# Last down projection of an attention and feed-forward block: two of seven products split by a second Strassen level, one-bank PSUM tiles

## The chip, the cores and the metric

The kernel runs on one core of a Trainium2 chip. The metric is the device time of one execution in microseconds (us); the time stated for a kernel is the median of its runs. A profile of one execution shows when each engine was busy and what ended its waits. The engines are TensorE (PE, matrix products into PSUM), VectorE (DVE), ScalarE (ACT), GpSimd (POOL) and SyncE (SP), whose queue issues most DMA transfers. "PEld" is the loading of a matmul's stationary operand.

## The reference

The inputs are bfloat16: x is 2048 x 1024, the gate and up weights are 1024 x 3584, the down weight is 3584 x 1024. Cut to what matters here:

```python
xn = layernorm(x)
s = linear_attention(xn, wqkv, wo)            # 32 heads, then @ wo
h = silu(xn @ w_gate) * (xn @ w_up)           # 2048 x 3584
g = silu(h @ w_down)                          # 2048 x 1024
out = x + s * g
```

## The kernel before

The attention part comes first (to about 246 us of the profile) and leaves `s` in DRAM. The feed-forward part then takes the 2048 tokens in two passes of 1024. A pass has a gate/up stage, which makes the hidden tile `h` (28 chunks of 128 hidden columns, each for 1024 tokens), and a down stage, which multiplies `h` by the down weight and finishes the output rows.

All of these products use one level of Strassen's scheme in Winograd's form. In the down stage, the left operand is cut into A11, A12 (tokens 0 to 511 with the even and the odd chunks of `h`) and A21, A22 (tokens 512 to 1023), the weight into B11, B12, B21, B22 with 512 output columns. Seven products take the place of eight: M1 = A11 B11, M2 = A12 B21, M3 = S4 B22, M4 = A22 T4, M5 = S1 T1, M6 = S2 T2, M7 = S3 T3, with S1 = A21 + A22, S2 = S1 - A11, S3 = A11 - A21, S4 = A12 - S2 and corresponding weight sums T. The outputs are C11 = M1 + M2, C21 = M1 + M6 + M7 + M4, C22 = M1 + M6 + M7 + M5, C12 = M1 + M6 + M5 + M3. The weight sums were made by POOL in the first pass (`emit_T`, L298) and lie in DRAM (`wd_drams`).

The last pass's down stage is `emit_down_m` (L1300). It takes the products one after another in the order 1, 2, 7, 6, 5, 4, 3 (`M_ORDER`, L190). Each covers four row tiles of 128 tokens; a row tile is 14 matmuls of 512 columns, accumulated into one PSUM bank (`prod_t`, L1337). Product 1 and 2 share banks; ACT copies the result of product 1 into the SBUF tile KA before product 2 goes on top. Products 6, 4 and the final pieces use four single-bank PSUM tiles (`pps`, "dx", L944); products 7, 5 and 3 use two tiles of two banks each (`ppd`, "dz", L945; `d_banks`, L1344). A bank's tile is what the dependency tracking knows: a wait counts for the whole tile. After a row tile, DVE adds KA or KB (`add`, L1352), ACT applies silu (`silu`, L1355), and `fin` (L1108) multiplies by `s` and adds `x` in two DVE operations, stores the rows through SP's queue, and asks for the `x` and `s` rows of a later tile (`io_load`, five tiles ahead).

The order on PE, DVE, ACT and POOL is the order in which the code emits the operations; SP's queue works in order too. Weights stream through eight slots of 1 MB (`w_slot`, L210, pool `wgu`, `NPK` = 8) in the order of `w_seq`; `load_w_to(n)` issues loads up to the n-th entry, and a load waits on SP until the slot's last reader is done. In the last gate/up stage the loop at L1518 asks for the tile of eight entries ahead of key i, makes products a and b of a key (`emit_a`, L964, `emit_b`, L997) and evacuates them on DVE and ACT (`emit_evac`, L1008). The loop also takes six `deferred` output tiles of the first pass, whose stores go through POOL's queue. POOL has no other work in this stage.

The end of the kernel is the last row tile of product 3, which is split into 384 and 128 columns (L1421 to L1437) so that silu, `fin` and store of the first piece run beside the second.

Of the kernel before, what the change touches and what calls it, by code (L numbers as in the profile page):

```python
# [21 lines left out]
def kernel(  # L22
# [12 lines left out]
    P = 128  # L35
# [152 lines left out]
    passes = list(range(NPASS - 1, -1, -1))  # L188
    NWA = NFG // 2
    M_ORDER = (1, 2, 7, 6, 5, 4, 3)  # L190
    M_PACK = {1: ("a", 3), 5: ("a", 0), 6: ("a", 1), 7: ("a", 2), 2: ("b", 0), 3: ("b", 1), 4: ("b", 2)}
    w_seq = []
    for p in passes:
        for fg in range(NFG):
            w_seq.append((p, "g", fg))
            w_seq.append((p, "u", fg))
        if p == passes[-1]:
            w_seq += [(p, "m", (M, hf)) for M in M_ORDER for hf in range(2)]
            continue
        for kd in ("a", "b"):  # L200
            for j in range(NWA):
                w_seq.append((p, kd, j))
# [13 lines left out]
    def load_wd(t, k):  # L216
        for c, q in ((2 * k, 3), (2 * k + 1, 0)):
            nc.sync.dma_start(out=wd_q(t)[:, q], in_=wd_v[:, c, :])

    def raw_view(key, t):  # L220
        return wd_q(t)[:, 0:4:3, :] if key[1] == "w" else t[:, 0].rearrange("p a b -> p (a b)")
# [8 lines left out]
    def load_w():  # L230
        key = w_seq[w_next[0]]
        w_next[0] += 1
        if key in w_tiles:
            return
        p, kind, k = key
        t = w_slot()
        if kind in ("a", "b"):
            src = wd_drams[k][0 if kind == "a" else 1]
            nc.sync.dma_start(out=t[:].rearrange("p h a b -> p (h a b)")[:, 0:2 * WDN[kind]],
                              in_=src[:].rearrange("p k q n -> p (k q n)"))  # L240
        elif kind == "m":
            (M, hf), (kd, q) = k, M_PACK[k[0]]
            v = wd_q(t).rearrange("p q n -> p (q n)").rearrange("p (k n) -> p k n", n=CW)
            for j in range(NWA):
                k0, k1 = max(2 * j, NWA * hf), min(2 * j + 2, NWA * (hf + 1))
                if k0 < k1:
                    nc.sync.dma_start(out=v[:, k0 - NWA * hf:k1 - NWA * hf],
                                      in_=wd_drams[j][0 if kd == "a" else 1][:, k0 - 2 * j:k1 - 2 * j, q])
        elif key[1:] in pk_drams:
            gate([nc.sync.dma_start(out=t[:], in_=pk_drams[key[1:]][:])], first_gate[0], sync=True)  # L250
        else:
            load_gu(t, kind, k, first_gate[0])
            raw_keys.add(key)
        w_tiles[key] = t
# [684 lines left out]
    with ExitStack() as p3:  # L939
# [1 line left out]
        m4 = p3.enter_context(tc.tile_pool(name="p3m", bufs=4, reuse_waits="tile"))  # L941
        iop = p3.enter_context(tc.tile_pool(name="p3io", bufs=5, reuse_waits="tile"))
        hp = p3.enter_context(tc.tile_pool(name="p3h", bufs=1, reuse_waits="tile"))
        pps = p3.enter_context(tc.tile_pool(name="p3ps", bufs=4, space=PSUM, reuse_waits="tile"))  # L944
        ppd = p3.enter_context(tc.tile_pool(name="p3pd", bufs=2, space=PSUM, reuse_waits="tile"))  # L945

        def k2(shape, dt, name):
            return kp.tile(shape, dt, name=name, tag="k2")
# [117 lines left out]
        def emit_hs(h, hf, m, eng):  # L1066
# [13 lines left out]
            eng.tensor_tensor(out=a21.bitcast(F16), in0=a12, in1=S2, op=ALU.subtract)  # L1080
            s_ring[(hf, m)] = (S1, S2, S3)

        deferred = []
        io_tiles = {}

# [32 lines left out]
        def emit_down(p, h, base, last, more_S, next_S):  # L1118
# [51 lines left out]
            def evac_a(t, keep):  # L1170
                x_, y_, zw = bk[t]
                if keep:
                    st = xnp.tile([P, 3, CW], FP32, name="kept", tag="xn8")
                    s1, s3, u4 = [st[:, q, :] for q in range(3)]
                else:
                    s1 = k2([P, CW], FP32, "s1")[:]
                    s3 = k2([P, CW], FP32, "s3")[:]
# [122 lines left out]
        def emit_down_m(p, h, base):  # L1300
# [3 lines left out]
            S1, S2, S4 = [v.bitcast(F16) for v in (A21, A11, A12)]  # L1304
            s3_ = [xnp.tile([P, NWA, TB], F16, name="S3h", tag="xn8") for _ in range(2)]
            EV = (nc.vector, nc.vector, nc.sync)

            def S3(k):
                return s3_[k // NWA][:, k % NWA]
# [4 lines left out]
                v = {1: A11, 2: A12, 3: S4, 4: A22, 5: S1, 6: S2}[M]  # L1314
                return lambda k: v[:, k]

            def sums(out, a, b_, op, part=slice(0, NFG)):
                for k in range(part.start, part.stop, 2):
                    nc.vector.tensor_tensor(out=out(k), in0=a[:, k:k + 2], in1=b_[:, k:k + 2], op=op)

            def at(v):
                return lambda k: v[:, k:k + 2]

            def s3_sums():
                for k in range(NFG):
                    nc.vector.tensor_tensor(out=S3(k), in0=A11[:, k], in1=A21[:, k], op=ALU.subtract)

            def w_of(M, k):
                t = w_tiles[(p, "m", (M, k // NWA))]
# [8 lines left out]
                for k in range(NFG):  # L1338
                    mm(M, t, k, out, first)

            def s_banks():
                return [pps.tile([P, CW], FP32, name="dx", tag="s")[:] for _ in range(TPB)]

            def d_banks():  # L1344
                v = [ppd.tile([P, 2, CW], FP32, name="dz", tag="d") for _ in range(TPB // 2)]
                return [v[t // 2][:, t % 2] for t in range(TPB)]

            def kept(nm):
                v = [m4.tile([P, 2, CW], FP32, name=nm, tag="m4") for _ in range(TPB // 2)]
                return [v[t // 2][:, t % 2] for t in range(TPB)]  # L1350

            def add(out, a, b_):  # L1352
                nc.vector.tensor_tensor(out=out, in0=a, in1=b_, op=ALU.add)

            def silu(c, nm):  # L1355
                g_ = k2([P, CW], BF16, nm)[:]
                nc.scalar.activation(out=g_, in_=c, func=ACT.Silu, scale=rch)
                return g_

            def load(n):  # L1360
                load_w_to(base + 2 * n + NPK)


            load(0)
            E = s_banks()
            KA = kept("kA")
            for t0 in (0, 2):
                for k in range(NFG):
                    for t in (t0, t0 + 1):
                        mm(1, t, k, E[t], True)  # L1370
                if t0 == 0:
                    s3_sums()
                for t in (t0, t0 + 1):
                    nc.scalar.copy(out=KA[t], in_=E[t])
            load(1)
            sums(at(S1), A21, A22, ALU.add)
            g = []
            for t in range(TPB):
                prod_t(2, t, E[t], False)
                g.append(silu(E[t], "g11"))  # L1380
                if t == 0:
                    sums(at(S2), S1, A11, ALU.subtract)
                else:
                    fin(p, t - 1, 0, g[t - 1], *EV)
            load(2)
            fin(p, TPB - 1, 0, g[-1], *EV)
            O = d_banks()
            KB = kept("kB")
            for t in range(TPB):
                prod_t(7, t, O[t], True)  # L1390
                add(KB[t], O[t], KA[t])
                if t == 0:
                    sums(at(S4), A12, S2, ALU.subtract)
            load(3)
            E = s_banks()
            for t in range(TPB):
                prod_t(6, t, E[t], True)
                add(KB[t], E[t], KB[t])
                add(KA[t], E[t], KA[t])
            load(4)  # L1400

            def out_of(M, bank, K, t, row, cc, pre):
                c = k2([P, CW], FP32, "c%d" % M)[:]
                add(c, bank, K)
                g_ = silu(c, "g%d" % M)
                if pre is not None:
                    fin(*pre, *EV)
                return (p, row, cc, g_)

            pre = None  # L1410
            O = d_banks()
            for t in range(TPB):
                prod_t(5, t, O[t], True)
                pre = out_of(5, O[t], KB[t], t, t + TPB, 1, pre)
            add(KA[-1], O[-1], KA[-1])
            E = s_banks()
            for t in range(TPB):
                prod_t(4, t, E[t], True)
                pre = out_of(4, E[t], KB[t], t, t + TPB, 0, pre)
            fin(*pre, *EV)  # L1420
            hs_ = [slice(0, 3 * CW // 4), slice(3 * CW // 4, CW)]  # L1421
            ps = [pps.tile([P, CW], FP32, name="df%d" % i, tag="s")[:] for i in range(2)]
            for i in range(2):
                nc.scalar.copy(out=ps[i][:, 0:hs_[i].stop - hs_[i].start], in_=KA[-1][:, hs_[i]])
            pre = None
            for t in range(TPB - 1):
                prod_t(3, t, O[t], False)
                pre = out_of(3, O[t], KA[t], t, t, 1, pre)
            fin(*pre, *EV)
            t = TPB - 1  # L1430
            g12 = k2([P, CW], BF16, "g12")[:]
            for i, cs in enumerate(hs_):
# [7 lines left out]
        for pi, p in enumerate(passes):  # L1440
# [68 lines left out]
                emit_hs(h, 0, 3, nc.vector)  # L1509

            na0 = 6 if first else 8
            load_w_to(base + na0)
            if first:
                wd_pipe2(-1)
# [1 line left out]
            emit_c22(keys[0])  # L1516
            first_gate[0] = None
            for i in range(n):  # L1518
                load_w_to(base + i + (na0 if i < n - 7 else 8 if i > n - 6 or not first else 7))
                if i + 1 < n:  # L1520
                    emit_a(keys[i + 1])
                    emit_c22(keys[i + 1])
# [19 lines left out]
                if first:  # L1542
                    wd_pipe2(i)
                    if i == 5:
                        emit_lk(0)
                    if i == n - 5:
                        emit_lam()
                    elif i == n - 4:
                        emit_sc(keys[-1], w_tiles[keys[-1]])
                        emit_T(keys[-1], w_tiles[keys[-1]])  # L1550
                        scale_h(h, 1, nc.vector)
                    elif i == n - 3:
                        scale_h(h, 3, nc.vector)
                if deferred:
                    deferred.pop(0)()
            base += n
# [37 lines left out]
```

## Time and profile before

| what | us |
|---|---|
| runs | 762.24, 762.67, 763.14 (median 762.67) |
| the profiled execution: its own time | 762.88 |
| its span, first to last instruction | 761.1 |
| last gate/up stage in it (about) | 500 to 667 |
| last down stage: first matmul, end of the last one | 667.70, 757.22 |
| last DVE operation ends | 758.24 |

The page of the profile gives the busy time of each engine, the chain of work that ended last, and groups of instructions by source line, engine and operation. A group's line ends with count, busy time, mean duration of one and the idle time before it with what ended it. Matmuls are pipelined: a matmul of 512 columns shows a duration of 379 ns, but 112 in a row take 24.17 us, 0.216 us each. A timeline lists instructions in order of time, equal neighbours merged; brackets give the engine's idle time before and what released it.

### The profile page before, as it was taken

To read this page: it belongs to the slowest core of one execution; us is meant where nothing else is said; L and a number is where in the kernel's file an instruction comes from. 1 tells how busy PE (TensorE), PEld (TensorE's weight loads), DVE (VectorE), ACT (ScalarE), POOL (GpSimd) and SP (SyncE) were. 2 spreads that over 40 slices of the span, in tenths; PEclk is the share of its full clock that TensorE was granted. 3 is DMA by queue.
4 is the path that set the end of the run, shared out by engine and by line. 5 is a ranking of instruction groups with operands and counts; after the bars stand their busy time and mean duration, and the time that the engine had idled before them with its cause. 6 is when DMAs were issued, how large, how long until landed. Compare 5 with 4: busy or idle time off the path is not lost.

```text
span 761.1 us, 10540 instructions
## 1 busy us (share of the span) xinstructions
PE 750.4 (99%) x3731; PEld 348.7 (46%) x3731; DVE 557.4 (73%) x1018; ACT 376.7 (50%) x529; POOL 273.9 (36%) x348
## 2 busy tenths in 40 slices
PE   8999999999999999999999999999999999999997
PEld 3544444454544444444444444444444444444443
DVE  6687787886796788888889755478767676794344
ACT  5678776988956566666659201142232322221012
POOL 2444799998540275867665000110000000000000
PEclk9999999999999999999999999999999999999999
DMA  9966799879679667888899046498545444565321
GB/s 316 303 148 132 236 329 306 292 159 296 203 160 311 221 237 269 310 295 306 268 349 404 30 150 236 152 399 283 195 176 186 185 168 146 174 205 180 99 90 49
DMA packets 117269, 170.31 MB, mean 224 GB/s; under 512 B 35488, under 2 KB 95392, under 8 KB 107488
## 3 DMA queue, kind: packets, MB, share of 16 engines
q1 hardware_dynamic: 111568, 144.99, 59.2%
q0 software_dynamic: 4208, 22.15, 7.5%
q10 hardware_dynamic: 1440, 2.49, 0.9%
q8 instruction: 29, 0.48, 0.2%
q14 instruction: 24, 0.20, 0.1%
HBM read 111.67 MB, written 50.59 MB: 213 GB/s over the span
## 4 chain that ended last, share of the span: by engine, by line
PE 96%; DVE 2%; ACT 1%; DMA 0%; issue 0%; ACTq 0%; DVEq 0%
PE zw L952 25%; PE kv_ps L541 15%; PE xb L952 13%; PE yb L952 6%; PE q_ps L183 6%; PE dzw L1140 6%; PE dx L1334 6%; PE dz L1334 4%; PE dx L1140 3%; PE fx L803 3%; PE s_ps L761 2%; PE dy L1140 2%; PE kvz L563 1%; PE nd L730 1%; DVE w_sb L296 0%; PE fx L761 0%
## 5 line engine op out<-in xcount | busy, mean ns | idle before, releaser
L952 PEld LDWEIGHTS <-w_sb 128*128 128x128 f16 (+1 forms) x1568 | 152.2, 98 | 182.7
L952 PE MATMUL xb<-xnT,w_sb 128*128 128x512 bf16 x448 | 115.0, 379 | 0.0
L541 PE MATMUL kv_ps<-wkv_sb,xnT 128*128 128x512 bf16 x512 | 113.7, 379 | 0.6 <-ACT xnT L530 0.4
L952 PE MATMUL zw<-xnT,w_sb 128*128 128x512 bf16 x448 | 105.8, 379 | 0.0
L952 PE MATMUL zw<-S,w_sb 128*128 128x512 f16 x448 | 105.8, 379 | 0.0
L308 POOL TENSOR_TENSOR w_sb<-w_sb 128x512 f16<-128x512 bf16 x42 | 50.2, 1195 | 95.7 <-DVE w_sb L296 51.3
L273 ACT ACTIVATE w_sb<-w_sb 128x2048 bf16<-128x2048 bf16 x42 | 79.9, 1902 | 4.6 <-DMA w_sb<-in_B_w_up_dram 4.6
L541 PEld LDWEIGHTS <-xnT 128*128 128x128 bf16 x512 | 48.4, 98 | 55.9 <-ACT xnT L530 0.8
L183 PE MATMUL q_ps<-xnT,wq_sb 128*128 128x512 bf16 x256 | 58.4, 379 | 0.0
L1028 ACT ACTIVATE sg<-cg 128x1024 bf16<-128x1024 f32 x28 | 29.6, 1057 | 57.4 <-DVE cg L1021 57.4
L952 PE MATMUL yb<-S,w_sb 128*128 128x512 f16 x224 | 57.4, 378 | 0.0
L1021 DVE SCALAR_TENSOR_TENSOR cg<-zw,rc_all,s 128x1024 f32<-128x1024 f32 x28 | 35.9, 1284 | 25.6 <-PE zw L952 13.8
L1334 PEld LDWEIGHTS <-hT 128*128 128x128 f16 (+1 forms) x350 | 33.7, 98 | 42.0 <-issue 3.2
L980 DVE SCALAR_TENSOR_TENSOR s<-yb,rc_all,s 128x512 f32<-128x512 f32 x42 | 31.4, 749 | 28.0 <-ACT s L979 28.0
L309 POOL TENSOR_TENSOR w_sb<-w_sb 128x512 f16<-128x512 bf16 x42 | 50.5, 1201 | 3.3
L311 POOL TENSOR_TENSOR w_sb<-w_sb 128x512 f16<-128x512 bf16 x42 | 50.3, 1197 | 0.0
L310 POOL TENSOR_TENSOR w_sb<-w_sb 128x512 f16<-128x512 bf16 x42 | 50.2, 1196 | 0.0
L1334 PE MATMUL dx<-w_sb,hT 128*128 128x512 bf16 (+1 forms) x224 | 48.8, 379 | 0.0
L1114 POOL DMA_DIRECT2D out_dram<-io x16 | 8.7, 542 | 101.9 <-DVE io L1113 101.6
L1140 PE MATMUL dx<-w_sb,hT 128*128 128x512 bf16 x112 | 42.4, 379 | 0.0
L979 ACT ACTIVATE s<-xb,rcl 128x512 f32<-128x512 f32 x14 | 9.6, 687 | 65.3 <-PE xb L952 65.3
L979 ACT ACTIVATE s<-xb,rc_all 128x512 f32<-128x512 f32 x42 | 28.3, 674 | 21.8 <-issue 12.8
(192 smaller groups left out, 1172.2 us busy)
## 6 DMA issues: line engine op xcount, KB each, us to landing
w_sb<-pk_g SPq DMA_DIRECT2D x27, 1024.0 KB, 5.5
pk_g<-w_sb SPq DMA_DIRECT2D x14, 1024.0 KB, 5.1
w_sb<-pk_u SPq DMA_DIRECT2D x14, 1024.0 KB, 5.0
pk_u<-w_sb POOLq DMA_DIRECT2D x13, 1024.0 KB, 5.4
w_sb<-wd SPq DMA_DIRECT2D x42, 256.0 KB, 3.8
w_sb<-in_B_w_gate_dram SPq DMA_DIRECT2D x14, 512.0 KB, 6.7
w_sb<-in_B_w_down_dram SPq DMA_DIRECT2D x28, 256.0 KB, 4.5
w_sb<-in_B_w_up_dram SPq DMA_DIRECT2D x14, 512.0 KB, 5.4
```

The costliest lines, as they stand in the source:

```text
L183: nc.tensor.matmul(q_ps[:], lhsT=wq_sb[:, dc, g * P:(g + 1) * P], rhs=xn_ap(dc, btok), start=(dc == 0), stop=(dc == DC - 1))
L273: nc.scalar.activation(out=junk, in_=raw_view(key, t), func=ACT.Square, accum_out=asum[:])
L308: nc.gpsimd.tensor_tensor(out=T1, in0=b12, in1=b11, op=ALU.subtract)
L309: nc.gpsimd.tensor_tensor(out=T2, in0=b22, in1=T1, op=ALU.subtract)
L310: nc.gpsimd.tensor_tensor(out=T3, in0=b22, in1=b12, op=ALU.subtract)
L311: nc.gpsimd.tensor_tensor(out=T4, in0=b21, in1=T2, op=ALU.subtract)
L541: mm = nc.tensor.matmul(kv_ps[:], lhsT=xn_ap(dc, tok), rhs=wkv_sb[:, dc, c * CW:(c + 1) * CW], start=(dc == 0), stop=(dc == DC - 1))
L952: mm = nc.tensor.matmul(out, lhsT=lhs(k), rhs=rhs(k), start=(first and k == 0), stop=(k == HK - 1), skip_group_check=True)
L979: nc.scalar.activation(out=s1[:], in_=x_[:], func=ACT.Copy, scale=rc)
L1021: nc.vector.scalar_tensor_tensor(out=d12, in0=zw[:], scalar=rc, in1=s2[:, None, :].to_broadcast([P, 2, TB]), op0=ALU.mult, op1=ALU.add)
L1140: nc.tensor.matmul(out, lhsT=lhs, rhs=rhs, start=first, stop=lastk, skip_group_check=True)
L1334: nc.tensor.matmul(out, lhsT=lhs_of(M)(k)[:, t * P:(t + 1) * P], rhs=w_of(M, k)[:, cols], start=first and k == 0, stop=k == NFG - 1, skip_ ...
```

## The change

Products 2 and 4 of the last down stage are each computed by a second level of the same scheme. For a pair of row tiles, the left operand (7 pairs of chunks) is a 2 x 2 grid: row tile by even or odd chunk; the weight is cut into two halves of 256 columns. Seven products of 128 rows, 7 chunks and 256 columns replace eight, for each of the two pairs (`l2_p`): 98 matmuls of 256 columns in place of 56 of 512. Results and partial results of a pair lie in halves of two banks (`l2_M`); ACT copies a half bank where a partial result is needed twice.

The second-level weight sums are made in the last gate/up stage: in every third key SP loads parts of the first-level sums into a weight slot (`l2_load`), POOL makes four differences (`l2_sums`) and stores seven blocks to DRAM (`l2_drams`). The weight lead in this stage is therefore six slots in place of eight until key 24. POOL also makes the left-hand sums for product 2 there (`l2_lhs`, every fourth key) and those for product 4 in the down stage, into two SBUF tiles left from the first pass. The weight entries of products 2 and 4 become four slots each (two of the seven products in one slot).

The PSUM pools of four single-bank and two two-bank tiles are closed before the down stage, and one pool of eight one-bank tiles takes their place. The order of the work changes with it: the first row tile of product 7 lies inside product 2, that of product 3 inside product 4; tile finishes are collected in a list (`fins`) and emitted by `flush`. The order of `w_seq` by products stays.

```diff
+    L2 = (2, 4)
+    L2_ORDER = (1, 5, 2, 6, 7, 4, 3)
-            w_seq += [(p, "m", (M, hf)) for M in M_ORDER for hf in range(2)]
+            w_seq += [(p, "m", (M, q)) for M in M_ORDER for q in range(4 if M in L2 else 2)]
...
+        def l2_load():
+            M, j0 = l2_q.popleft()
+            kd, q = M_PACK[M]
+            t = w_slot()
+            v = t[:].rearrange("p h a b -> p (h a b)").rearrange("p (b j n) -> p b j n", b=8, n=CH)
+            js = range(j0, min(j0 + 2, NQ))
+            for j in js:
+                for k, b0, b1 in ((0, 0, 7), (1, 2, 6)):
+                    src = wd_drams[j][0 if kd == "a" else 1][:, k, q].rearrange("p (c n) -> p c n", n=CH)
+                    nc.sync.dma_start(out=v[:, b0:b1 + 1:b1 - b0, j - j0, :], in_=src)
...
+            for o_, a_, b_ in ((1, 7, 0), (3, 6, 1), (4, 6, 7), (5, 2, 3)):
+                nc.gpsimd.tensor_tensor(out=b(o_), in0=b(a_), in1=b(b_), op=ALU.subtract)
+            nc.gpsimd.dma_start(out=l2_drams[M][:, :, js.start:js.stop, :], in_=v[:, 0:7, 0:n_, :])
...
+            eng.tensor_tensor(out=s1, in0=a21, in1=a22, op=ALU.add)
+            eng.tensor_tensor(out=s2, in0=s1, in1=a11, op=ALU.subtract)
+            eng.tensor_tensor(out=s3, in0=a11, in1=a21, op=ALU.subtract)
+            eng.tensor_tensor(out=s4, in0=a12, in1=s2, op=ALU.subtract)
...
+            p3a.close()
+            ppm = p3.enter_context(tc.tile_pool(name="p3m8", bufs=2 * TPB, space=PSUM, reuse_waits="tile"))
...
+                for i, r in ((1, 0), (5, 0), (1, 1), (5, 1)):
+                    l2_p(M, i, r, A, bk)
+                for r in range(2):
+                    nc.scalar.copy(out=zy(r)[:, hi], in_=xw(r)[:, lo])
+                for r in range(2):
+                    l2_p(M, 2, r, A, bk)
+                    l2_p(M, 6, r, A, bk)
+                    nc.scalar.copy(out=zy(r)[:, lo], in_=zy(r)[:, hi])
+                    tt(K[2 * r][:, hi] if in_place else c[r][0][:, hi], zy(r)[:, hi], K[2 * r][:, hi])
+                for r in range(2):
+                    l2_p(M, 7, r, A, bk)
...
+                fill()
+                for r in range(2):
+                    l2_p(M, 4, r, A, bk)
...
+                    l2_p(M, 3, r, A, bk)
...
+            bk = banks()
+            E = [bk[2], bk[3], bk[0], bk[1]]
...
+            l2_M(4, quads(h, 1, 1), KB, done4, fill3, True)
+            out3(1)
+            flush(len(fins) - 1)
...
+            out3(2)
+            flush()
...
-                load_w_to(base + i + (na0 if i < n - 7 else 8 if i > n - 6 or not first else 7))
+                    load_w_to(base + i + (6 if i < 3 * len(l2_steps) else 8))
...
+                    if i % 3 == 0 and l2_q:
+                        l2_load()
+                    if i % 3 == 1 and l2_live:
+                        l2_sums()
+                    if i % 4 == 0 and i >= 4:
+                        l2_lhs(quads(h, 1, 0), i // 4 - 1, nc.gpsimd)
```

## The prediction

> **What bounds the kernel now.** I read the table of busy time by stage first, with stages cut at the last pass's borders, then the chain of waits of the last stage, then that stage's timeline engine by engine, and last the single rows that price the new operations. TensorE (PE) is busy 99% of the span, so the question is where in the last down projection it isn't streaming.
>
> ```profile
> span 761.1 us, 10540 instructions
> PE 750.4 (99%) x3731; PEld 348.7 (46%) x3731; DVE 557.4 (73%) x1018; ACT 376.7 (50%) x529; POOL 273.9 (36%) x348
> ...
> 246.00:415.00 169.00, 169.00 (x803) 76.79 (x801) 142.41 (x237) 110.68 (x123) 111.11 (x111) 1.00 0.82 293
> ...
> 500.00:667.00 167.00, 167.00 (x775) 75.73 (x774) 123.97 (x151) 50.64 (x72) 3.24 (x6) 1.00 0.58 208
> 667.00:761.10 94.10, 86.31 (x411) 39.38 (x408) 48.86 (x96) 15.05 (x24) 0.00 (x0) 0.99 0.38 123
> ```
>
> The columns are the stretch, its length, then busy us of PE, PE's weight loads, DVE, ACT, POOL, then PE clock, DMA share and GB/s. Row one is the first pass's gate/up stage, row two the last pass's, row three the last down stage. PE is full in both gate/up stages; POOL is idle in the last two. In the last stage PE loses 7.8 us, and the chain says where:
>
> ```profile
> 667.87 24.17 PE dx L1334 x112
> 692.04 3.04 PE dz L1334 x14
> 695.08 0.02 issue
> 695.10 0.70 DVE kB L1353
> 695.80 0.04 issue
> 695.85 6.22 PE dz L1334 x28
> ```
>
> The columns are start, length, what. After each first tile of a product in the two-bank "dz" tiles PE stands until a DVE addition has read that bank, because the second bank belongs to the same tile. It happens five times (695.1, 702.1, 721.1, 728.1, 747.2). By issue times one costs more than the 0.78 us shown idle:
>
> ```profile
> 691.88 3.19 PE L1334 MATMUL dz<-w_sb,S3h 128*128 128x512 f16 x14
> 695.85 6.20 PE L1334 MATMUL dz<-w_sb,S3h 128*128 128x512 f16 x28 [0.78 <-DVE kB L1353]
> ```
>
> **Part 1: 112 matmuls of 512 columns become 196 of 256.** Products 2 and 4 are 56 matmuls each now; 112 take 24.17 us in the chain, 0.216 each. Two-level, each is 7 products x 2 row tiles x 7 chunks = 98 matmuls of 256 columns. No 256-column row exists. Below, half of 0.216 is 0.108. Above, a matmul of 384 columns: the last product's first 14 take 2.29 us, 0.1636 each. Its last 14, of 128 columns, run from 756.45 to 757.22, 0.055 each, though every weight load lasts 98 ns: loads hide even there. The middle of 0.055 and 0.1636 is 0.109, which I take, as 256 lies between these two rows. 196 x 0.109 = 21.4, a gain of 2.8 us. Bounds: 3.0 us gained (0.108) or 7.9 lost (0.1636).
>
> ```profile
> 754.16 2.29 PE df L1334 x14
> 756.45 0.02 issue
> ...
> 757.26 0.37 ACT L1436 ACTIVATE g<-df,hsc 128x128 bf16<-128x128 f32 x1 [0.20 <-PE df L1334]
> ```
>
> The Trainium skill, "TensorE: Matmul & The Clock Gate", section Back-to-back issue gap, speaks against this: it gives streams of weight load plus matmul a sustained 81 ns at 128 columns and says the plain N/2.4 + 2.5 ns under-counts small ones. If its 26 ns excess over this trace's 55 held at 256 columns, 196 x 0.026 = 5.1 us would more than eat the gain and the sum would read 763.4. The same section gives 131 ns at 512, where this trace has 216; the measurement decides.
>
> **Part 2: the five stalls.** The 14 matmuls from 691.88 would end their issue 3.02 us later; PE restarts 3.97 later: 0.95 lost. The pair from 695.85 restarts after 6.98 instead of 6.04: 0.94. Five make 4.7 us. With one-bank tiles the next tile of products 7, 5 and 3 waits for no evacuation of its neighbour, so I count all 4.7.
>
> **Part 3: what PE waits for instead.** (a) The new pool of one-bank tiles gives the second tile of product 1 a bank of the last "zw" pair. Its second matmul so waits for DVE's last evacuation:
>
> ```profile
> 667.90 1.28 DVE L1021 SCALAR_TENSOR_TENSOR cu<-zw,rcl,s 128x1024 bf16<-128x1024 f32 x1 [0.65 <-PE zw L952]
> ```
>
> It ends at 669.18; with a hand-over of 0.06 (695.79 to 695.85 above) PE goes on at 669.24 where it would have issued at 667.92: 1.32 us lost. All 55 matmuls left of that half-product's stream, and every later one, stand behind it. (b) In products 2 and 4, the third group (product 7 of the second row pair) waits for an ACT copy of half a bank and then a DVE addition from the same bank. The copies of 128 and 384 columns take 0.253 and 0.470, so 256 about 0.36; the additions of 512 and 1024 columns take 0.69 and 1.22, so 256 about 0.43. With hand-overs of 0.03, 0.03 and 0.06 and 0.16 until the last result lands (379 ns duration against 0.216 pitch) the chain is 1.07 us; the first pair's seven matmuls cover 0.76. 0.31 lost, twice: 0.6. Bounds: 0 (copy and addition overlap) and 2.1 (no cover). Less than nothing is excluded, since nothing before this group gets shorter.
>
> **Part 4: the tail.** DVE's stores are put off: after product 4 six output tiles wait to be multiplied and stored ("fin": two DVE operations each), and five of them are queued between the additions of tiles 1 and 2 of product 3. A burst in the pass before prices one:
>
> ```profile
> 481.70 0.42 DVE L1112 TENSOR_TENSOR g<-g,io 128x512 bf16<-128x512 bf16 x1
> 482.15 0.42 DVE L1113 TENSOR_TENSOR io<-g,io 128x512 bf16<-128x512 bf16 x1
> 482.50 0.42 DVE L1112 TENSOR_TENSOR g<-g,io 128x512 bf16<-128x512 bf16 x1
> ```
>
> 0.80 each. Counted from tile 1's result: addition to 0.64, five fins to 4.64, addition of tile 2 to 5.33, its silu on ACT (0.72) to 6.08, the fin before it to 6.05, its own to 6.91, the two last pieces (1.15, as from 757.09 to 758.24) to 8.06. PE is done 3.02 + 2.29 + 0.77 = 6.08 after the start, so DVE ends 1.98 behind PE, against 1.02 now (757.22 to 758.24). 1.0 us lost; bounds 0, and 1.8 if a fin takes the 0.93 it has here when each waits for its silu. The inputs of the burst's first fin are asked for behind the store of the fin in product 4's middle, 0.3 + 1.7 + 0.8 + 3.4 = 6.2 us (issue, landing, two issues, landing), some 8 us ahead. The stores (1.7 us to landing) and the end behind the last one stay.
>
> **Part 5: costed at nothing.** POOL gets, in the last gate/up stage, 32 sums on weights and 28 on activations, and 28 more in the down stage, for which it has until product 4's second group. At 1.2 us a 128x512 sum (its rows: 1195 to 1201 ns) and about 0.7 for half of that, 54 us fit in 167; the last 28 need 20 us and have 33. SP issues 28 more loads of 128 KB in that stage and 8 fewer for products 2 and 4; POOL issues 8 more stores, and six leftover output stores of the first pass stand behind its sums, with SP's reloads behind those and the gate/up weights behind them on SP. The cover is lead: with 6 slots ahead a weight tile is asked for four keys of 167/28 = 5.96 us, 24 us, before use, and lands in 5.5. A POOL step (4 x 1.2 + 0.6 = 5.4 us) is inside it. DMA grows by about 12.8 MB, 77 GB/s over 208, near the first gate/up stage's 293, where no PE wait is listed. Without this cover each us late is a us on the end. DVE's other sums move but end 4 us or more before PE needs them: after product 2 DVE owes seven sums of 0.61 us, and product 6, which reads them, is three tiles (9.1 us) away. With the stalls gone DVE has 3.0 us a tile for at most 2.1 us of additions and fin, so nothing is late next there.
>
> Here the Trainium skill, "SBUF — State Buffer", on the shared port pair, warns that a DVE operation with two SBUF inputs and a GpSimd operation block each other for a whole instruction. In this trace DVE's hT product keeps 952 to 959 ns whether POOL is busy 111 us of the stage or 3; only POOL stretches, 1142 to 1600 ns in one row.
>
> **Sum.** PE: -2.8 - 4.7 + 1.3 + 0.6 = -5.6. Tail: +1.0. Together -4.6 on the profiled execution's own 762.88 us (span 761.1 and 1.8 around it), which lies 0.2 above the median of 762.67 and inside the runs' 762.24 to 763.14: 758.3.
>
> **The rivals.** *Half-width matmuls cost more than half* (slower). One mechanism, the pitch in products 2 and 4: at 0.1325 the gain is gone, from 0.140 on the kernel is slower by over 0.2%, at 0.1636 it ends at 769.0. For it: no such matmul in the trace. Against: 0.055 at 128 columns under the same loads. Chance 0.07. *POOL takes DVE's time in the last gate/up stage*: 54 us of sums, if each held DVE, against 43 us of DVE idle: 11 over, 769. Against: the first gate/up stage, with twice the POOL work and a fuller DVE. Slower from 6 us over. Chance 0.06. *New waits and tail at their upper bounds*: +1.5 and +0.8, 760.6, still faster; additions on busy queues speak for it. Chance 0.16. *The stalls stay* (another dependency takes the bank's place): 763.0, no change. The order of waits speaks against it. Chance 0.07. *The forecast*: 0.64.
>
> About 0.2% (1.5 us) is what a measurement can tell from no change. Faster: 0.64 + 0.16 = 0.80; the same: 0.07 and a little of the first rival, 0.08; slower 0.12. The range: low 756.9, (b) and the tail near zero; high 761.6, beyond the upper waits and into the first rival at a pitch of 0.126.
>
> **What the profile after would show.** Right: 196 matmuls on one line with about 272 ns each and 98 of them in 10.7 us; no 0.78 us gap behind a kB or c addition; one 1.1 to 1.3 us PE gap behind "cu" just after the last gate/up matmul; two of about 0.3 behind the l2c and kB additions; DVE ending 2 us after PE; PE full in the last gate/up stage with POOL near 57 us. Wrong: the 98 taking 12 us or more; a PE wait on POOL or on a weight load; DVE ending 3 us behind.

## The result, and the profile after

The changed kernel takes 758.0 us in the median of four runs (757.58 to 758.68), the kernel before 762.89 in the same series: a ratio of 0.9938 (95% interval 0.9921 to 0.9955). A second series gave 757.94 (five runs) and 0.9935 (0.9921 to 0.9949). The forecast was 758.3. The profiled execution took 757.71 us, its span is 755.9.

The head of the profile of the changed kernel:

```profile
span 755.9 us, 10887 instructions
PE 746.6 (99%) x3815; PEld 356.8 (47%) x3815; DVE 573.5 (76%) x1036; ACT 379.5 (50%) x537; POOL 361.1 (48%) x444
```

The same stages as before, after the change (stretch, length, then busy us of PE, its weight loads, DVE, ACT and POOL, then PE clock, DMA share and GB/s):

```profile
246.00:415.00 169.00, 169.00 (x803) 76.78 (x802) 143.25 (x237) 110.92 (x124) 111.27 (x111) 1.00 0.81 291
500.00:667.00 167.00, 166.67 (x773) 75.54 (x772) 126.38 (x150) 50.49 (x72) 60.79 (x70) 1.00 0.75 267
667.00:755.90 88.90, 82.87 (x493) 47.45 (x491) 64.37 (x113) 16.82 (x32) 27.35 (x32) 1.00 0.52 165
```

POOL now works 61 us in the last gate/up stage and 27 us in the last down stage. PE is idle for 6.0 us of the last row, most of it behind its last matmul. And it is no longer full in the last gate/up stage: 0.33 us are missing, which the forecast did not have. The chain of waits of the last stage, after the change (start, length, what):

```profile
667.57 1.29 DVE cu L1035
668.86 0.04 issue
668.90 12.03 PE dm L1400 x55
680.93 6.13 PE dm L1433 x56
687.06 0.02 issue
687.08 0.37 ACT dm L1455
687.45 0.02 issue
687.47 0.44 DVE l2c L1388
687.91 0.04 issue
687.95 0.92 PE dm L1433 x7
688.88 3.02 PE dm L1400 x14
691.90 3.06 PE dm L1433 x28
694.95 33.24 PE dm L1400 x154
```

The pieces behind "kB" and "c" additions in the middle of a product are gone: 154 matmuls of products 7, 6, 5 run as one piece of 33.24 us. In their place stand the two waits that the forecast named: "cu" ahead of product 1's second matmul, and ACT's copy with DVE's addition ahead of the third group of product 2 (product 4 shows the same at 734.34). The 56 matmuls of 256 columns take 6.13 us, 0.109 each.

I cut the last part of each profile at three points: the first matmul of the last gate/up stage (498.49 us before, 497.66 after), the first matmul of the down stage (667.70 and 667.36) and the end of DVE's last operation (758.24 and 753.41). Before, the gate/up stage takes 169.21 us and the down stage 90.54; after, 169.70 and 86.05. The down stage got 4.49 us shorter, the gate/up stage 0.49 longer. The rest of the 5.2 us of span lies elsewhere: the code ahead of 498 us, which the change does not touch, ended 0.83 sooner, and the time from there to the last record of the trace fell from 2.84 to 2.53 us. The first of the two is a difference between executions: over all profiles of this study that point lies between 497.66 and 498.98. I therefore compare stages below, and use whole times as a check. That the whole came within 0.3 us of the forecast is in part luck: the sum has neither this difference, nor the shorter end, nor the loss in the gate/up stage, and the last offsets part of the others.

Two of the signs that the forecast named look otherwise: the waits on half banks show 0.14 us of idle time each, not 0.3 (by the starts of the matmuls on both sides they cost 0.30, since 0.41 us lie there in place of 0.11), and PE is not full in the last gate/up stage, where POOL has 61 us in place of 57.

### The profile page after: what moved, and what is told of

It is laid out like the page before. It is cut to its first block, busy times and chain, and to the rows that moved or that the text cites. A ratio compares the mean times of both kernels' runs of the same rounds, so it can differ in the third digit from the quotient of the medians.

```text
span 755.9 us, 10887 instructions
## 1 busy us (share of the span) xinstructions
PE 746.6 (99%) x3815; PEld 356.8 (47%) x3815; DVE 573.5 (76%) x1036; ACT 379.5 (50%) x537; POOL 361.1 (48%) x444
## 4 chain that ended last, share of the span: by engine, by line
PE 96%; DVE 2%; issue 1%; DMA 0%; ACT 0%; DVEq 0%; ACTq 0%
PE zw L966 25%; PE kv_ps L554 15%; PE xb L966 12%; PE q_ps L183 7%; PE dm L1400 7%; PE dzw L1204 6%; PE yb L966 6%; PE dx L1204 3%; PE s_ps L774 3%; PE fx L816 3%; PE dm L1433 3%; PE dy L1204 2%; PE nd L743 1%; PE kvz L576 1%; DVE g L1176 1%
## 5 line engine op out<-in xcount | busy, mean ns | idle before, releaser
L1122 POOL TENSOR_TENSOR w_sb<-w_sb 128x512 f16<-128x512 bf16 (+3 forms) x32 | 34.6, 1103 | 61.0 <-DMA w_sb<-wd 52.3
L1400 PE MATMUL dm<-w_sb,hT 128*128 128x512 f16 (+3 forms) x238 | 49.2, 366 | 1.2 <-DVE cu L1035 1.2
```

Of the source, the lines that this page charges most:

```text
L1400: nc.tensor.matmul(out, lhsT=lhs_of(M)(k)[:, t * P:(t + 1) * P], rhs=w_of(M, k)[:, cols], start=first and k == 0, stop=k == NFG - 1, skip_ ...
```

## The experiments

My theory is the sum on record: five gaps gone (-4.7), half-width matmuls (-2.8), the cu wait (+1.3), two half-bank waits (+0.6), the tail (+1.0). The rival to it is that the gain has one source, with the other terms as by-products. A second question is the 0.49 us in the gate/up stage, which none of these terms has.

| kernel | time, us (median) | ratio to before, 95% interval | last gate/up stage, us | down stage to DVE's end, us | behind it, us |
|---|---|---|---|---|---|
| before (its first profile) | 762.67 to 763.09 | 1 | 169.21 | 90.54 | 2.84 |
| changed (first series) | 758.0 | 0.9938 (0.9921 to 0.9955) | 169.70 | 86.05 | 2.53 |
| changed, once more | 757.94 | 0.9935 (0.9921 to 0.9949) | 169.22 | 86.03 | 2.55 |
| one-bank tiles only | 759.58 | 0.9955 (0.9942 to 0.9967) | 169.22 | 87.14 | 2.82 |
| one-bank tiles, product 1 by tiles | 758.18 | 0.9938 (0.9925 to 0.9950) | 169.21 | 85.83 | 2.82 |
| changed, product 1 by tiles | 757.07 | 0.9920 (0.9908 to 0.9933) | 169.71 | 84.72 | 2.54 |
| changed, tail dealt out | 757.21 | 0.9924 (0.9912 to 0.9936) | 169.21 | 84.96 | 2.54 |
| changed, 60 of POOL's sums left out | 758.69 | 0.9939 (0.9925 to 0.9953) | 169.21 | 86.03 | 2.86 |
| all three losses mended | 755.04 | 0.9898 (0.9885 to 0.9912) | 169.27 | 83.06 | 2.54 |
| the same, sums begun later | 755.17 | 0.9899 (0.9886 to 0.9913) | 169.22 | 83.05 | 2.54 |

**The one-bank tiles alone.** The products stay as before; only the pools change.

```diff
-        pps = p3.enter_context(tc.tile_pool(name="p3ps", bufs=4, space=PSUM, reuse_waits="tile"))
-        ppd = p3.enter_context(tc.tile_pool(name="p3pd", bufs=2, space=PSUM, reuse_waits="tile"))
+        p3a = ExitStack()
+        pps = p3a.enter_context(tc.tile_pool(name="p3ps", bufs=4, space=PSUM, reuse_waits="tile"))
+        ppd = p3a.enter_context(tc.tile_pool(name="p3pd", bufs=2, space=PSUM, reuse_waits="tile"))
...
-            def s_banks():
-                return [pps.tile([P, CW], FP32, name="dx", tag="s")[:] for _ in range(TPB)]
-            def d_banks():
-                v = [ppd.tile([P, 2, CW], FP32, name="dz", tag="d") for _ in range(TPB // 2)]
...
+            p3a.close()
+            ppm = p3.enter_context(tc.tile_pool(name="p3m8", bufs=2 * TPB, space=PSUM, reuse_waits="tile"))
+            def s_banks(n=TPB):
+                return [ppm.tile([P, CW], FP32, name="dm", tag="m")[:] for _ in range(n)]
+            d_banks = s_banks
...
-            E = s_banks()
+            bk = s_banks()
+            E = [bk[2], bk[3], bk[0], bk[1]]
...
```

> The kernel before, with its products as they are (512 columns, no second level), and only the PSUM pools of the last down stage exchanged for one pool of eight one-bank tiles, as the change has it. Theory (parts 2 and 3a of the prediction): the five gaps of 0.78 us behind kB and c additions go, five times 0.94 to 0.95 of issue is 4.7 us gained; the second matmul of product 1 now waits for the last cu evacuation, 1.3 us lost; together -3.4, so 759.5 us against the 762.9 of the kernel before, and the changed kernel is only about 1.3 us faster than this one (half-width matmuls -2.8, waits on half banks +0.6, tail +1.0). Rival: the gain of the change comes from the half-width products, the gaps are a matter of DVE and stay or move: no more than 1 us faster than before.

It took 759.58 us, and its down stage 87.14, 3.40 less than before. The chain of waits of this kernel:

```profile
667.74 1.30 DVE cu L1022
669.03 0.04 issue
669.08 83.82 PE dm L1335 x391
752.89 0.02 issue
752.92 0.59 ACT g L1439
```

After the cu wait PE streams to the end without a stop. The rival falls: the gaps were a matter of the two-bank tiles, and most of the gain is there without any second level. The changed kernel's down stage is 1.1 us shorter than this one's, near the 1.2 that the other terms sum to (-2.8 + 0.6 + 1.0).

**Product 1 tile by tile**, so that the bank of the last zw pair is needed 14 matmuls later.

```diff
-                for k in range(NFG):
-                    for t in (t0, t0 + 1):
-                        mm(1, t, k, E[t], True)
+                for t in (t0, t0 + 1):
+                    prod_t(1, t, E[t], True)
```

> The changed kernel with product 1 computed tile after tile instead of two tiles alternating, so that the bank which the last zw pair held is first needed 14 matmuls (3.0 us) later than now. Theory (part 3a): the 1.3 us gap behind the last cu evacuation goes and nothing takes its place: last stage 1.3 us shorter than the changed kernel's 83.95 us from its first matmul to PE's end, 756.6 us in all. Rival: the gap only moves, because product 1's first tile then also waits for a bank that is evacuated late (an ACT copy or the cu itself): no change.

The down stage took 84.72 us, 1.33 less than the changed kernel's 86.05, and the time was 757.07. The chain of waits across the border, in this kernel:

```profile
666.73 1.73 PE zw L966 x8
668.46 12.09 PE dm L1400 x56
```

The cu evacuation has left the chain; product 1 follows the last gate/up matmul. Against the kernel before in its own series the median gains 6.02 us, where the changed kernel gained 4.89. The two profiled executions differ by 0.3 us only (757.40 and 757.71), because this one began its last gate/up stage 0.92 us later; both have a gate/up stage of 169.7.

**The tail dealt out.**

```diff
+            flush(2)
             out3(1)
-            flush(len(fins) - 1)
+            flush(3)
```

> The changed kernel with the five held-back output tiles of the tail dealt out differently: two are finished before product 3's tile 1 is issued (so ahead of its addition in DVE's queue) and three after it, instead of five between the additions of tiles 1 and 2. Theory (part 4): DVE's lag behind PE at the end falls from 2.1 us to about 1.0, what the kernel before has, and the time by 1.0 to 756.9 us. Rival: the lag is that of the last tile's own chain (silu, two multiplications, two last pieces) and not of the burst: no change, or the burst is only met earlier and holds a PE bank.

In the changed kernel, the timeline of DVE (start, length, operation, and in brackets the idle time before it) ends with no idle moment from the addition of tile 2 on:

```profile
749.92 0.68 DVE L1388 TENSOR_TENSOR c<-dm,kA 128x512 f32<-128x512 f32 x1
750.52 0.41 DVE L1176 TENSOR_TENSOR g<-g,io 128x512 bf16<-128x512 bf16 x1
...
752.26 0.35 DVE L1176 TENSOR_TENSOR g<-g,io 128x384 bf16<-128x384 bf16 x1
752.65 0.36 DVE L1177 TENSOR_TENSOR io<-g,io 128x384 bf16<-128x384 bf16 x1
752.92 0.22 DVE L1176 TENSOR_TENSOR g<-g,io 128x128 bf16<-128x128 bf16 x1
753.18 0.23 DVE L1177 TENSOR_TENSOR io<-g,io 128x128 bf16<-128x128 bf16 x1
```

PE's last matmul ends at 751.31 there, so DVE is 2.10 us behind. With the tail dealt out:

```profile
751.41 0.36 DVE L1176 TENSOR_TENSOR g<-g,io 128x384 bf16<-128x384 bf16 x1 [0.50 <-ACT g L1568]
751.80 0.36 DVE L1177 TENSOR_TENSOR io<-g,io 128x384 bf16<-128x384 bf16 x1
752.08 0.22 DVE L1176 TENSOR_TENSOR g<-g,io 128x128 bf16<-128x128 bf16 x1
752.33 0.22 DVE L1177 TENSOR_TENSOR io<-g,io 128x128 bf16<-128x128 bf16 x1
```

DVE waits for the last tile's silu again, ends 1.02 us behind PE (751.53), as in the kernel before, and the down stage takes 84.96 us, 1.09 less. The lag came from the burst.

**POOL's sums left out.** The 32 sums on weights and the 28 for product 4's left operand go, so this kernel does not compute these operands; the 28 for product 2 stay, and so do matmuls, evacuations and stores. POOL's busy time in the last gate/up stage falls from 60.8 to 26.8 us.

```diff
-                for k, b0, b1 in ((0, 0, 7), (1, 2, 6)):
+                for k, b0, b1 in ((0, 0, 7), (1, 2, 6), (0, 1, 3), (1, 4, 5)):
...
-                nc.gpsimd.tensor_tensor(out=b(o_), in0=b(a_), in1=b(b_), op=ALU.subtract)
+                pass
...
-            for j in range(NQ):
-                l2_lhs(quads(h, 1, 1), j, nc.gpsimd)
```

> The changed kernel with POOL's second-level sums left out: the four differences of weight blocks in every step of the last gate/up stage (the blocks are loaded as they are, by two more loads a step) and the second round of sums on activations in the down stage (product 4 takes product 2's sums). So this kernel does not compute those operands; its matmuls, evacuations and stores are those of the changed kernel. Theory: the sums of POOL slow DVE operations with two inputs beside them (0.42 us fins at 1.26 to 1.36 in the last gate/up stage, 0.69 us sums at 1.1 in the down stage), which costs a PE wait of 0.33 us and some 0.5 us of that stage and nothing in the down stage, where DVE has room: DVE's durations fall back, the gate/up stage falls from 169.7 to 169.2 us and the time by 0.5 to 757.5 us. Rival: the 0.5 us is run to run difference of the stage and has nothing to do with POOL: DVE durations may fall, the time doesn't. Second rival: POOL's sums cost in the down stage too: 1 us or more.

This answered half. DVE's durations fell back as the theory had it, but for one hT product of 1.20 us in the last gate/up stage, where product 2's sums are still made. Groups of DVE instructions in the down stage (line, operation, shapes, count, busy us, mean ns, idle us before), of the changed kernel:

```profile
L1388 DVE TENSOR_TENSOR hT<-hT 128x1024 f16<-128x1024 bf16 x14 | 11.4, 881 | 0.0
...
L1388 DVE TENSOR_TENSOR hT<-hT 128x1024 f16<-128x1024 f16 x7 | 7.4, 1125 | 0.0
```

and without POOL's sums:

```profile
L1388 DVE TENSOR_TENSOR hT<-hT 128x1024 f16<-128x1024 bf16 x14 | 8.6, 679 | 0.0
...
L1388 DVE TENSOR_TENSOR hT<-hT 128x1024 f16<-128x1024 f16 x7 | 4.3, 684 | 0.0
```

The gate/up stage was 169.21 us, with no PE wait, and the down stage 86.03, the same as with the sums: there DVE has room, so the second rival falls. But the time did not fall: 758.69 us, not 757.5. This profile reached the gate/up stage at 498.98, 1.32 later than the first profile of the changed kernel and 0.62 later than the second, and ended 2.86 us behind DVE, 0.3 more than the other kernels with the second level. The first lies ahead of the edit, the second behind the stages that it touches (more on it below). From whole times alone the first rival would have won; whether the sums cost 0.5 us had to be settled in another way.

**The changed kernel once more**, as it is.

> The changed kernel as it is, once more, beside the other kernels of this series. Theory (the 0.5 us that the last gate/up stage got longer is DVE's two-input operations beside POOL's sums, and depends on how these fall together): the stage takes 169.2 to 169.7 us again, with some of DVE's three last held-back multiplications above 1 us, and the last stage from its first matmul to DVE's end again 86.0 us; time 758.0 give or take 0.7, which is how far the start of the first gate/up stage moved between profiles of code that is the same up to there. Rival: the first gain was partly luck of one series, and the time is 759.5 or more.

757.94 us, and the gate/up stage took 169.22. So the 0.5 us is not there in every execution. The first profile of the changed kernel shows the wait; from its timelines of DVE, and then of PE, in the last gate/up stage:

```profile
520.65 1.36 DVE L1176 TENSOR_TENSOR g<-g,io 128x512 bf16<-128x512 bf16 x1
522.04 1.26 DVE L1177 TENSOR_TENSOR io<-g,io 128x512 bf16<-128x512 bf16 x1
```

```profile
527.51 0.81 PE L966 MATMUL zw<-S,w_sb 128*128 128x512 f16 x3 [0.33 <-DVE cu L1035]
```

In the second profile, the timelines of POOL and then of DVE over the same stretch:

```profile
520.17 5.02 POOL L1122 TENSOR_TENSOR w_sb<-w_sb 128x512 f16<-128x512 bf16 x4 [9.20 <-PE zw L966]
```

```profile
520.15 1.28 DVE L1035 SCALAR_TENSOR_TENSOR cg<-zw,rc_all,s 128x1024 f32<-128x1024 f32 x1 [0.67 <-PE zw L966]
521.35 0.42 DVE L1176 TENSOR_TENSOR g<-g,io 128x512 bf16<-128x512 bf16 x1
521.80 1.26 DVE L1177 TENSOR_TENSOR io<-g,io 128x512 bf16<-128x512 bf16 x1
523.13 0.75 DVE L994 SCALAR_TENSOR_TENSOR s<-yb,rc_all,s 128x512 f32<-128x512 f32 x1
```

The last held-back tile of the pass before is multiplied and added here, 0.84 us when POOL is quiet. Beside POOL's sums the pair took 1.78 us longer than that in the first profile (1.36 + 1.26 - 0.84) and the stage lost 0.49; in the one with product 1 by tiles 1.79 longer and 0.50 lost; in the mended kernel 1.35 and 0.06; with the tail dealt out 1.22, and here 0.84, and nothing lost. All five profiles fit a slack of DVE of about 1.3 us at this place, the loss being what goes beyond it. How the pair falls against POOL's four sums differs from execution to execution: in the second profile the multiplication began 0.05 us before POOL's second sum and kept its 0.42 us, while that sum took 1.38 us in place of 1.15; in the first profile it began 0.08 us after a sum and took 1.36.

**All three losses mended at once.** Besides the two edits above, 5 of the 14 matmuls of each fill tile move ahead of the third group:

```diff
-            def prod_t(M, t, out, first):
-                for k in range(NFG):
+            def prod_t(M, t, out, first, ks=range(NFG)):
+                for k in ks:
...
+            KS = (range(0, 5), range(5, NFG))
...
+                fill(0)
                 for r in range(2):
                     l2_p(M, 7, r, A, bk)
...
-                fill()
+                fill(1)
...
```

> The changed kernel with product 1 tile after tile, with the tail's output tiles dealt two and three around product 3's tile 1, and with each fill tile of products 2 and 4 split: 5 of its 14 matmuls stand before the seven of the third group (product 7 of the second row pair), 9 behind. Theory: the three losses of the change are independent and add up: 1.33 (cu wait) + 1.09 (tail) + 2 x 0.29 (third group, now covered by 1.08 us of other matmuls) = 3.0 us less in the last stage than the changed kernel, 83.1 us from first matmul to DVE's end, and about 755.0 us in all. Rival: they overlap: with PE 1.9 us earlier DVE is late again at the end, and only 2 us or less are gained.

755.04 us; the down stage took 83.06. Its chain of waits:

```profile
680.01 6.11 PE dm L1435 x56
686.13 1.08 PE dm L1400 x5
687.21 1.53 PE dm L1435 x14
688.74 1.94 PE dm L1400 x9
690.68 3.06 PE dm L1435 x28
693.74 33.24 PE dm L1400 x154
```

ACT's copy and DVE's addition have left the chain. Of the 2.99 us below the changed kernel, 1.33 and 1.09 are the two terms measured singly; the 0.57 left are the two half-bank waits, 0.29 each (0.30 by the starts of the matmuls). They add up, and the rival of an overlap falls.

**One-bank tiles with product 1 by tiles, no second level.** The edit is that of the second experiment, made in the kernel of the first.

> The kernel with one-bank tiles and 512-column products (no second level), and product 1 tile after tile. Theory: the cu wait goes here too, 1.33 us: last stage 85.8 us from first matmul to DVE's end, time about 758.2, as good as the changed kernel that has the second level and all of POOL's sums. The second level then is worth what its matmuls save, 2.7 to 2.8 us, and no more: that is what this kernel has to differ by from the one with all three losses mended (83.1 in the last stage). Rival: one of the two gains of the change is not there without the other: this kernel differs from the mended one by less than 2 or more than 3.5 us.

758.18 us and a down stage of 85.83: what the changed kernel reaches, without second level and without POOL's sums. The mended kernel's stage is 2.77 us shorter than this one's. Neither has a wait of PE in the down stage and both end 1.02 us behind PE, so these 2.77 us are the half-width matmuls by themselves, against 2.8 forecast.

**POOL's sums begun later**, in the mended kernel.

```diff
-                    load_w_to(base + i + (6 if i < 3 * len(l2_steps) else 8))
+                    load_w_to(base + i + (6 if i < 3 + 3 * len(l2_steps) else 8))
...
-                    if i % 3 == 0 and l2_q:
+                    if i >= 3 and i % 3 == 0 and l2_q:
```

> The kernel with all three losses mended, and POOL's sums on weight blocks begun three keys (18 us) later in the last gate/up stage, behind DVE's held-back multiplications of the pass before. Theory: these multiplications keep 0.42 us each, no PE wait behind cu at 527, and the gate/up stage takes 169.2 us; gain up to 0.5 us over the mended kernel where that one had the wait, none where it had not. Rival: the wait comes from elsewhere (a late weight block, the hT product alone) and stays; or product 4's weights, summed last, now come late: a wait of PE in the last stage.

From DVE's timeline in this kernel:

```profile
521.59 0.42 DVE L1176 TENSOR_TENSOR g<-g,io 128x512 bf16<-128x512 bf16 x1
522.04 0.43 DVE L1177 TENSOR_TENSOR io<-g,io 128x512 bf16<-128x512 bf16 x1
```

The pair keeps its 0.84 us, the gate/up stage takes 169.22, and no weight comes late in the down stage (83.05). The time is 755.17 us against 755.04: no difference, as the mended kernel's own profile had lost only 0.06 here. The edit takes away a loss that comes in some executions; these runs don't show a gain from it.

## Why the prediction was right, and where it was not

- *Part 1, half-width matmuls, -2.8:* right, 2.77 measured. All 196 matmuls of 256 columns last 269 to 273 ns with a pitch of 0.109 us, the middle of the 128- and 384-column rows. The Trainium skill, "TensorE: Matmul & The Clock Gate", Back-to-back issue gap, gives a sustained 81 ns at 128 columns, whose excess would have eaten the gain; this trace does not agree with that. The N/2.4 + 2.5 ns of the same section, there the gap of an isolated matmul, gives an estimate of 109.2 ns at 256 columns, and the trace agrees with that.
- *Part 2, the five stalls, -4.7:* right. The kernel with one-bank tiles and product 1 by tiles has neither them nor the cu wait and its down stage is 4.71 us shorter than before. Pricing them by issue times (0.94 to 0.95) and not by the idle time shown (0.78, which would give 3.9) made this term.
- *Part 3a, the cu wait, +1.32:* right; 1.33 came back when it was taken away, and 1.31 in the kernel without second level.
- *Part 3b, the half-bank waits, +0.6:* right, 0.57 for both.
- *Part 4, the tail, +1.0:* right, 2.10 us behind PE against 1.98 forecast; 1.09 came back.
- *Part 5, costed at nothing:* the step that failed is "DVE's hT product keeps 952 to 959 ns whether POOL is busy 111 us of the stage or 3; only POOL stretches". DVE does stretch: 0.42 to 1.37 us in the worst case here. The error was to compare totals of a stage. In the first gate/up stage the hT product and POOL's sums hardly meet; from the first stage's timeline of the changed kernel:

```profile
271.32 1.15 POOL L324 TENSOR_TENSOR w_sb<-w_sb 128x512 f16<-128x512 bf16 x1
272.56 0.96 DVE L1047 TENSOR_TENSOR hT<-cu,sg 128x1536 bf16<-128x1536 bf16 x1
272.79 0.57 POOL L339 DMA_DIRECT2D pk_u<-w_sb  x1 [0.31 <-POOL w_sb L324]
273.38 1.17 POOL L321 TENSOR_TENSOR w_sb<-w_sb 128x512 f16<-128x512 bf16 x1
```

  They share 0.14 us here, at most 0.34 in this stage, and wherever it is more than 0.03 the hT product began first, kept its 0.96, and the sum was the one to stretch (at 0.34 shared, 1.35 us in place of 1.15). In the last pass they share whole operations, with POOL's sum the first to begin, and the hT product takes up to 1.99 us. The cost of the step is 0 to 0.5 us, by how the two meet, far from the rival's 11 us; the rest is covered by DVE's slack, which the forecast had not counted at that place. The rule of the skill that the forecast set aside ("SBUF — State Buffer", on the shared port pair) was the better guide. The forecast also put the growth of the DMA traffic too high: 77 GB/s over 208, where the profile shows 267, 59 more; no wait came of it.

Of the sum, -4.6, the down stage shows -4.49 and -4.51 in the two profiles. The second profile's span is 4.9 us below the one before: of the other 0.4 us, 0.1 lies ahead of the last gate/up stage and 0.3 behind DVE's last operation, 2.84 to 2.55. The forecast had that end as unchanged. The kernels with the second level have 2.53 to 2.55 there, except the one without POOL's sums (2.86), the others 2.82 to 2.84. The records of SP's queue in the traces show where it goes: at the end SP passes nine semaphore waits one after another, some 0.06 us apart where nothing is left to wait for. In the kernels with the long end the waits that end as the last two stores land are the third and fourth, and five more follow; in those with the short end they are the seventh and eighth, and one follows. Four waits are 0.24 us, and the last store lands 0.05 to 0.07 us sooner (1.57 us behind DVE in place of 1.62 to 1.63). What sets the order of these waits was not tried and stays open.

## What to carry to other kernels

Price a stall by the issue times on both sides of it, and when it goes, ask which buffer the freed engine asks for next and who held it last: here 1.9 us of 7.5 went back into new waits, and 1.0 more into a burst of held-back work, all removable by order alone. Split the cheap edit from the clever one: the one-bank tiles with a reordered product gave, without the second level, what the whole change gave with it. And a figure that an operation keeps "beside" another engine is evidence only where their timelines overlap, and one has to see which of the two began first.

## What the runs showed of the chip that I had not expected

- DVE operations with both inputs in SBUF stretch beside POOL's sums that began before them (0.42 to as much as 1.37 us for 128x512 in bf16; 0.96 to as much as 1.99 for 128x1536; 0.684 to 1.125 in the mean for 128x1024 in f16), while those that read a PSUM tile do not: in the fence of the second profile above, the cg evacuation lies on POOL's sums for 1.19 us and takes 1.28, as it does elsewhere, and the next takes 0.75.
- The same code ahead of the last gate/up stage ended anywhere between 497.66 and 498.98 us over ten profiles. A difference of half a microsecond between two kernels could only be read from the stage, not from the whole.
